# Lightning attention feeding a leaky-ReLU feed-forward block: the attention's small matmuls gathered into one TensorE visit per chunk, with the PSUM banks shared out anew

## The chip, the cores and the metric

One core of one Trainium2 chip runs the whole program. The metric is the device time of that core in microseconds (us): 662.45 us as the median of three runs of the kernel before (660.42 to 664.43). A separately profiled execution of it spans 662.8 us; all profile times below are counted from the start of that span.

## The reference

Two blocks follow each other. The attention works on blocks of 64 tokens with a decaying state; its output, 3072 tokens by 512 features, is the input of a feed-forward block with a leaky ReLU.

```
batch, heads, seq, head_dim = 4, 8, 768, 64          # block = 64 tokens
for each block b:
    intra = (q_b k_b^T * Dmask) v_b                   # within the block
    inter = (q_b * lam_pow) kv_state                  # from the blocks before
    out_b = intra + inter
    kv_state = lam**64 * kv_state + (k_b * rev_pow)^T v_b
x = out as (3072 tokens, 512)
h = x @ w_in            # 512 x 2048
g = max(0.01 h, h)
return g @ w_out        # 2048 x 512
```

The weights arrive as 64-bit floats and are converted on the chip.

## The kernel before

**Three products for one.** A 32-bit product is built from three products of TensorE's shorter 32-bit type (fp32r). An operand x is split into a high part xh and a rest xl, and a third operand xm is made of the two; the same for w. The first two products, h with h and l with l, are summed in one PSUM bank (`b1`), the third, m with m, goes to another (`b2`), and ScalarE and VectorE put the two sums together. For one half (`f`) of a pair of feature blocks `p` and one group `g` of 512 tokens this is 3 x 4 matmuls of 128x128 weights by 512 columns:

```python
def up(g, p):                                  # first layer, one of 48 steps
    ...
    for f in range(2):
        t, r = tt[jt], gs[jg][:, f, :]
        add("PE", 0.91, lambda f=f: product(b1, f, 0, True), keys("h"), ["b1"])     # 4 matmuls
        add("PE", 0.91, lambda f=f: product(b1, f, 1, False), keys("l"), ["b1"])    # 4 matmuls
        add("ACT", 0.6, lambda t=t: nc.scalar.activation(out=t, in_=b1, func=AF.Copy, ..., scale=1.0 + 1.0 / S), ["b1"], [f"t{jt}"])
        add("PE", 0.91, lambda f=f: product(b2, f, 2, True), keys("m"), ["b2"])     # 4 matmuls
        add("DVE", 0.69, lambda t=t, r=r: nc.vector.tensor_tensor(r, t, b2, op=ALU.add), [f"t{jt}", "b2"], [f"gs{jg}"])
    ...                                        # leaky ReLU on ScalarE, store to memory
```

**A planner in the kernel.** `add` only records an operation with its engine, a duration the author assumes, and the keys it reads and writes. At the end `plan.emit()` plays the list through, engine by engine, and emits the instructions in the order of that play. Each engine then runs its instructions in this fixed order; only semaphores hold it.

**Attention by chunks of 128 tokens** (24 chunks, two blocks each). A "quad" is a 64x64 by 64x64 matmul on a quarter of the array.

```python
pt = [ps([P, HP, C], f"pt{i}") for i in range(2)]      # two banks: transposes of k and q, later the state updates
psc = ps([P, 2, 2 * HP, C2], "psc")                    # two banks, scores in the lower half of each
po = ps([P, 2, 2 * HP, C2], "po")                      # two banks, outputs in the lower half of each
b1, b2 = ps([P, T], "b1"), ps([P, T], "b2")            # one bank each

def attention(c):
    ...                                                # loads of k, q, v (two buffers each)
    transposed(tk, 0, "k", kT)                         # PE: 4 transposes, ACT copies them out
    transposed(tq, 1, "q", qT)                         # PE: 4 transposes, ACT copies them out
    add("POOL", 1.15, ...)                             # k *= decay
    add(...)                                           # q * powers of lam
    add("PE", 0.56, scores, ...)                       # 16 quads into psc
    add("DVE", 0.69, ...)                              # sc = psc * mask
    add("PE", 0.56, kv, ...)                           # 16 quads: state updates, into pt[0], pt[1]
    add("PE", 0.56, own, ["sc", f"v{i}"], ["po"])      # 16 quads
    ...                                                # state = state + update (DVE), state * lam**64 (POOL)
    for n in range(2):
        add("PE", 0.3, lambda n=n: inter(n), ..., ["po"], rank=1.5 * n)      # 8 quads each
        if n == 0:
            add("DVE", 0.15, lambda: nc.vector.tensor_copy(seen_po, po[:, :, 0, 0]), ["po"], ["seen_po"])
    add("ACT", 0.6, ... scale=S)                       # xs = S * po
    add("ACT", 0.6, ... scale=NEAR)                    # xh = po rounded to fp32r
    add("DVE", 0.75, ...)                              # xl = xs - S * xh   (both from SBUF)
    add(("DVE", "POOL"), (0.75, 1.2), ... ALU.subtract)   # xm = xh - xl      (either engine)
```

Each of these PE entries is placed by itself, wherever the planner finds its inputs ready, between entries of `up`. The weights' parts `wl` may also be computed by either VectorE or GpSimd (`("DVE", "POOL"), (1.3, 2.3)`).

**Order of the whole.** Chunks 0 to 3 come first; then 48 steps `up(g, p)` with the other 20 chunks between them, in bursts of four as the two buffers of X come free; the eight w_in conversions lie ahead of the first steps, and the eight w_out conversions beside later ones; then the second layer (`down`), 1152 more matmuls of the same size.

Of the kernel before, what the change touches and what calls it, by code (L numbers as in the profile page):

```python
# [23 lines left out]

S = 4096.0
NEAR = 1.0 - 2.0 ** -13

# [6 lines left out]
class Plan:  # L34
# [6 lines left out]
    def __init__(self):  # L41
        self.ops, self.last, self.rank = [], {}, 0.0

    def add(self, eng, us, fn, reads=(), writes=(), rank=0.0):

        n, deps = len(self.ops), set()
        for k in reads:
            w, r = self.last.setdefault(k, [None, []])
            if w is not None:
                deps.add(w)  # L50
            r.append(n)
        for k in writes:
            w, r = self.last.setdefault(k, [None, []])
            if w is not None:
                deps.add(w)
            deps.update(r)
            self.last[k] = [n, []]
        deps.discard(n)
        ways = {eng: us} if isinstance(eng, str) else dict(zip(eng, us))
        self.ops.append((ways, fn, deps, (self.rank + rank, n)))  # L60

    def emit(self):
        n = len(self.ops)
        left = [len(o[2]) for o in self.ops]
# [20 lines left out]
        while len(done) < n:  # L85
            best = None
            for e in free:
                for i in able[e]:
                    t = max(free[e], since(i, e))
# [3 lines left out]
            ways, fn = self.ops[i][:2]  # L93
            for x in ways:
                able[x].discard(i)
# [15 lines left out]
def kernel(  # L111
# [39 lines left out]
    pt = [ps([P, HP, C], f"pt{i}") for i in range(2)]  # L151
    psc = ps([P, 2, 2 * HP, C2], "psc")
    po = ps([P, 2, 2 * HP, C2], "po")
    b1, b2 = ps([P, T], "b1"), ps([P, T], "b2")
# [3 lines left out]
    xs = [sb([P, KO, C], f"xs{i}") for i in range(2)]  # L158
# [35 lines left out]
    for _ in range(WARM):  # L194
        nc.tensor.transpose(out=b1[:, 0:P], in_=ident, identity=ident)
# [39 lines left out]
    def attention(c):  # L235
        b, s0, i = c // NCB, (c % NCB) * C, c % 2
        first, last = c % NCB == 0, c % NCB == NCB - 1
        tk, tq, tv = (x[i] for x in kqv)
        kT, qT, qsT = kTs[i], qTs[i], qsTs[i]

        pu = [(b1.rearrange("p (y t) -> p y t", y=HP), "b1"), (b2.rearrange("p (y t) -> p y t", y=HP), "b2")] if c < GC else [
            (pt[0], "pt0"), (pt[1], "pt1")]

        def load(src, dst, nm):
            y = src[b, :, s0:s0 + C, :]
            if nm == "v":
                add("DMA", 1.15, lambda: nc.sync.dma_start(out=dst, in_=y.rearrange("h p d -> p h d")), [], [f"v{i}"])
            else:
                def go():
                    for z in range(2):  # L250
                        nc.sync.dma_start(out=dst[:, z * HP:(z + 1) * HP, :], in_=y[z::2].rearrange("h p d -> p h d"))  # L251
                add("DMA", 1.15, go, [], [f"{nm}{i}"])

        for src, dst, nm in ((k, tk, "k"), (q, tq, "q"), (v, tv, "v")):
            load(src, dst, nm)

        def transposed(src, z, nm, into):
            def go():
                for y in range(HP):
                    nc.tensor.transpose(out=pt[z][:, y, :], in_=src[:, 2 * y:2 * y + 2, :].rearrange("p a d -> p (a d)"),  # L260
                                        identity=ident)
            add("PE", 0.45, go, [f"{nm}{i}"], [f"pt{z}"])
            add("ACT", 0.6, lambda: nc.scalar.copy(into, pt[z]), [f"pt{z}"], [f"{nm}T{i}"])

        transposed(tk, 0, "k", kT)
        transposed(tq, 1, "q", qT)
        kr = tk.rearrange("p (y x) d -> p y x d", x=2)
        nr = slice(0, C2 if last else P)
        add("POOL", 1.15, lambda: nc.gpsimd.tensor_tensor(kr[nr], kr[nr], _bc(pow_k, 3, D)[nr], op=ALU.mult),  # L269
            ["fk"], [f"k{i}"])  # L270

        m = slice(1 if first else 0, 2)
        o, x = (z.rearrange("p y (t i) -> p y t i", t=2)[:, :, m, :] for z in (qsT, pt[1] if c < GC else qT))
        eng, e, us, src = ("DVE", nc.vector, 0.7, "pt1") if c < GC else ("POOL", nc.gpsimd, 1.4, f"qT{i}")
        add(eng, us, lambda: e.tensor_tensor(o, x, _bc(pow_q, 2, 2)[:, :, m, :], op=ALU.mult), ["fq", src], [f"qsT{i}"])

        def scores():
# [4 lines left out]

        add("PE", 0.56, scores, [f"kT{i}", f"qT{i}"], ["psc"])
        add("DVE", 0.69, lambda: nc.vector.tensor_tensor(sc, psc[:, :, 0:HP, :], decay, op=ALU.mult), ["psc", "fk"], ["sc"])  # L284

        n_pu = 1 if last else 2

        def kv():
            for y in range(HP):
                for x in range(2):  # L290
                    for t in range(n_pu):
                        h = y // 2 + (2 * y + x) % HP * 2
                        quad(pu[t][0][:, y, 0:D], t, tk[:, 2 * y + x, :], tv[:, h, :], x, start=y == 0)

        add("PE", 0.56, kv, [f"k{i}", f"v{i}"], [pu[t][1] for t in range(n_pu)])
# [9 lines left out]
        def inter(n):  # L305
            for y in range(HP):
                t = y % 2 ^ n
                for hi in range(2):
                    if not first or t:
# [3 lines left out]
        add("PE", 0.56, own, ["sc", f"v{i}"], ["po"])  # L313
        for t in range(n_pu):
            j = 2 * c + t
            new = state[j % 4]
            if first and t == 0:
                add("DVE", 0.42, lambda new=new: nc.vector.tensor_copy(new, pu[0][0][:, :, 0:D]), [pu[0][1]], [f"st{j % 4}"])
            else:
                add("DVE", 0.42, lambda new=new, t=t: nc.vector.tensor_tensor(new, new, pu[t][0][:, :, 0:D], op=ALU.add),  # L320
                    [pu[t][1]], [f"st{j % 4}"])
            if not last:
                add("POOL", 0.7, lambda new=new, j=j: nc.gpsimd.tensor_tensor(state[(j + 1) % 4], new, _bc(lam_c, 2, D), op=ALU.mult),  # L323
                    [f"st{j % 4}", "fq"], [f"st{(j + 1) % 4}"])
            if t == 0:
                for n in range(2):
                    add("PE", 0.3, lambda n=n: inter(n), [f"qsT{i}", f"st{j % 4}"] + ([] if first else [f"st{(j - 1) % 4}"]), ["po"],
                        rank=1.5 * n)
                    if n == 0:

                        add("DVE", 0.15, lambda: nc.vector.tensor_copy(seen_po, po[:, :, 0, 0]), ["po"], ["seen_po"])
# [4 lines left out]
        y = po[:, :, 0:HP, :]  # L336
# [4 lines left out]
        def name(x):  # L341
            return f"x{x}{g % 2}"

        add("ACT", 0.6, lambda: nc.scalar.activation(out=tok(xs[i]), in_=y, func=AF.Copy, bias=0.0, scale=S), ["po"], [f"xs{i}"])
        add("ACT", 0.6, lambda: nc.scalar.activation(out=tok(xh), in_=y, func=AF.Copy, bias=0.0, scale=NEAR),  # L345
            ["po"], [name("h") + str(cc)])
        add("DVE", 0.75, lambda: nc.vector.scalar_tensor_tensor(xl, xh.bitcast(F32), -S, xs[i], op0=ALU.mult, op1=ALU.add),  # L347
            [name("h") + str(cc), f"xs{i}"], [name("l") + str(cc)])
# [226 lines left out]
```

## Time and profile before

| what | value |
|---|---|
| time, median of three | 662.45 us |
| TensorE busy (matmul) | 637.4 us, 96% |
| VectorE, ScalarE, GpSimd busy | 54%, 43%, 14% |
| first-layer matmuls (line 432) | 3 x 384, from 35.3 us on |
| second-layer matmuls (line 482) | 12 groups of 96 |
| transposes (line 260), quads (line 225) | 192 and 1472 + 768 + 576 + 128 records (two per quad) |
| mean granted TensorE clock | 0.983 of full; 0.86 in the first 50 us, 0.93 in the next 50, 1.00 after |

How to read it: matmuls overlap one another, and their ends are modelled, so the busy share of TensorE says little; the distance from one matmul's start to the next one's start says more. That distance is read from the timeline, whose lines give start, length, engine, source line, what is written from what, and how many instructions in a row were merged. An "idle before" in brackets names what ended a wait. "PEld" is the loading of weights into the array. A quad leaves two records, so x32 is 16 quads.

### The profile page before, as it was taken

How to read it: one execution, taken by the hardware profiler on the slowest of the kernel's cores; microseconds unless marked ns; L12 is line 12 of the kernel's file. 1: busy time of each engine (PE TensorE's matmuls, PEld its weight loads, DVE VectorE, ACT ScalarE, POOL GpSimd, SP SyncE). 2: the span in 40 equal slices, each digit the busy share in tenths (PEclk: the TensorE clock that was granted, in tenths of full speed). 3: DMA queues.
4: the chain of work that ended last, by engine and by line, in shares of the span. 5: the costliest groups of instructions: out<-in, count | busy, mean ns of one | idle time of the engine just before them, and what ended most of it. 6: DMA issues, size and time to landing. Idle time of an engine off the chain costs nothing.

```text
span 662.8 us, 13107 instructions
## 1 busy us (share of the span) xinstructions
PE 637.4 (96%) x5450; PEld 505.2 (76%) x5450; DVE 359.9 (54%) x481; ACT 285.8 (43%) x412; POOL 93.2 (14%) x96
## 2 busy tenths in 40 slices
PE   6688999999999999999999999999999999999997
PEld 5565767877677777777777778888888888888885
DVE  5777887555666234324326788363554544554631
ACT  5555778776776344453443353222231312222211
POOL 2542522311242124222200000000000000000000
PEclk8887999999999999999999999999999999999999
DMA  8855676877786435333243565252333332423201
GB/s 209 223 156 150 191 213 220 253 237 250 223 245 191 163 112 144 114 118 106 75 181 133 186 225 188 93 186 68 144 114 125 119 135 84 171 94 129 96 0 63
DMA packets 102090, 101.51 MB, mean 153 GB/s; under 512 B 78480, under 2 KB 78480, under 8 KB 102032
## 3 DMA queue, kind: packets, MB, share of 16 engines
q1 hardware_dynamic: 101888, 100.68, 48.5%
q8 instruction: 42, 0.69, 0.4%
q14 instruction: 16, 0.13, 0.1%
q10 hardware_dynamic: 144, 0.00, 0.0%
HBM read 65.02 MB, written 35.65 MB: 152 GB/s over the span
## 4 chain that ended last, share of the span: by engine, by line
PE 85%; DMA 4%; DVE 3%; ACT 3%; issue 2%; SPq 1%; POOL 0%; ACTq 0%; DVEq 0%; POOLq 0%
PE b L432 37%; PE po L482 10%; PE psc L482 10%; PE pt L482 10%; PE b L482 10%; PE po L225 3%; PE pt L260 2%; DMA raw<-in_moe_w_in_dram 2%; PE psc L225 2%; DMA wo<-w 1%; PE pt L225 1%; SPq L251 1%; DMA att<-in_v_dram 1%; DVE w L385 1%; DVE xm L349 1%
## 5 line engine op out<-in xcount | busy, mean ns | idle before, releaser
L446 DVE TENSOR_TENSOR gs<-t,b 128x512 f32<-128x512 f32 x96 | 65.8, 686 | 105.3 <-PE b L432 80.5
L432 PE MATMUL b<-xh,wh 128*128 128x512 f32 x384 | 114.4, 420 | 4.0 <-ACT xh L345 2.5
L467 ACT ACTIVATE xh<-att 128x1024 fp32r<-128x1024 f32 x48 | 50.8, 1061 | 144.1 <-PE po L482 141.0
L432 PE MATMUL b<-xm,wm 128*128 128x512 f32 x384 | 105.7, 398 | 4.7 <-DVE gs L446 3.1
L468 DVE SCALAR_TENSOR_TENSOR xl<-xh,att 128x1024 fp32r<-128x1024 f32 x48 | 58.6, 1221 | 93.7 <-ACT xh L467 93.7
L432 PE MATMUL b<-xl,wl 128*128 128x512 f32 x384 | 106.1, 398 | 0.9 <-DVE xl L347 0.9
L443 ACT ACTIVATE t<-b 128x512 f32<-128x512 f32 x96 | 57.2, 596 | 96.9 <-PE b L432 96.5
L432 PEld LDWEIGHTS b<-xm,wm 128*128 128x128 f32 x384 | 72.1, 190 | 21.2 <-DVE gs L446 3.5
L432 PEld LDWEIGHTS b<-xl,wl 128*128 128x128 f32 x384 | 71.6, 189 | 18.3 <-DVE xl L347 1.8
L432 PEld LDWEIGHTS b<-xh,wh 128*128 128x128 f32 x384 | 65.6, 190 | 23.7 <-ACT t L443 8.9
L448 ACT ACTIVATE gs<-gs 128x1024 f32<-128x1024 f32 x48 | 50.8, 1059 | 31.8 <-DVE gs L446 31.8
L470 DVE TENSOR_TENSOR xm<-xh,xl 128x1024 fp32r<-128x1024 f32 x48 | 58.8, 1225 | 4.8
L225 PEld LDWEIGHTS po<-att 64*64 64x64 f32 x1472 | 28.7, 140 | 24.2 <-issue 12.2
L225 PE MATMUL po<-att 64*64 64x64 f32 x1472 | 36.3, 231 | 6.2 <-DVE att L284 2.4
L269 POOL TENSOR_TENSOR att<-att 128x512 f32<-128x512 f32 (+1 forms) x24 | 27.9, 1161 | 100.0 <-PE pt L260 90.6
L323 POOL TENSOR_TENSOR att<-att 128x256 f32<-128x256 f32 x40 | 29.8, 746 | 73.0 <-DVE att L320 55.9
L482 PE MATMUL psc<-wm,xm 128*128 128x512 f32 x96 | 37.3, 389 | 0.0
L482 PE MATMUL po<-wh,xh 128*128 128x512 f32 x96 | 37.3, 389 | 0.0
L482 PE MATMUL pt<-wh,xh 128*128 128x512 f32 x96 | 37.3, 389 | 0.0
L482 PE MATMUL psc<-wl,xl 128*128 128x512 f32 x96 | 37.3, 389 | 0.0
L482 PE MATMUL b<-wl,xl 128*128 128x512 f32 x96 | 37.3, 389 | 0.0
L482 PE MATMUL b<-wm,xm 128*128 128x512 f32 x96 | 37.3, 389 | 0.0
(76 smaller groups left out, 935.0 us busy)
## 6 DMA issues: line engine op xcount, KB each, us to landing
g<-gs SPq DMA_DIRECT2D x48, 512.0 KB, 3.1
att<-g SPq DMA_DIRECT2D x48, 512.0 KB, 3.2
raw<-in_moe_w_in_dram SPq DMA_DIRECT2D x16, 512.0 KB, 4.5
raw<-in_moe_w_out_dram SPq DMA_DIRECT2D x16, 512.0 KB, 4.0
att<-in_k_dram SPq DMA_DIRECT2D x48, 128.0 KB, 3.3
att<-in_q_dram SPq DMA_DIRECT2D x48, 128.0 KB, 3.0
att<-in_v_dram SPq DMA_DIRECT2D x24, 256.0 KB, 3.7
out_dram<-gs SPq DMA_DIRECT2D x24, 256.0 KB, 2.2
```

What stands on the lines that cost most here:

```text
L225: nc.tensor.matmul(dst[HALF[cols]], lhsT=lhsT[HALF[rows]], rhs=rhs[HALF[rows]], start=start, stop=True, skip_group_check=True)
L260: nc.tensor.transpose(out=pt[z][:, y, :], in_=src[:, 2 * y:2 * y + 2, :].rearrange("p a d -> p (a d)"), identity=ident)
L269: add("POOL", 1.15, lambda: nc.gpsimd.tensor_tensor(kr[nr], kr[nr], _bc(pow_k, 3, D)[nr], op=ALU.mult), ["fk"], [f"k{i}"])
L323: add("POOL", 0.7, lambda new=new, j=j: nc.gpsimd.tensor_tensor(state[(j + 1) % 4], new, _bc(lam_c, 2, D), op=ALU.mult), [f"st{j % 4}", "f ...
L432: nc.tensor.matmul(dst, lhsT=w[z][:, kk * 2 * P + f * P:kk * 2 * P + (f + 1) * P], rhs=x[z][:, kk, :], start=start and kk == 0, stop=kk == ...
L443: add("ACT", 0.6, lambda t=t: nc.scalar.activation(out=t, in_=b1, func=AF.Copy, bias=0.0, scale=1.0 + 1.0 / S), ["b1"], [f"t{jt}"], rank=-1.5)
L446: add("DVE", 0.69, lambda t=t, r=r: nc.vector.tensor_tensor(r, t, b2, op=ALU.add), [f"t{jt}", "b2"], [f"gs{jg}"], rank=-1.5)
L448: add("ACT", 1.05, lambda: nc.scalar.activation(out=y, in_=y, func=AF.Prelu, bias=0.0, scale=S, alpha=0.01), [], [f"gs{jg}"], rank=-1.5)
L467: add("ACT", 1.05, lambda: nc.scalar.activation(out=h, in_=graw[j], func=AF.Copy, bias=0.0, scale=NEAR / S), reads, wr("h"))
L468: add("DVE", 1.3, lambda: nc.vector.scalar_tensor_tensor(l, h.bitcast(F32), -S, graw[j], op0=ALU.mult, op1=ALU.add), reads + [f"rh{j}"], w ...
L470: add(("DVE", "POOL"), (1.3, 2.3), lambda e: ENG[e].tensor_tensor(m, h.bitcast(F32), l.bitcast(F32), op=ALU.subtract), [f"rh{j}", f"rl{j}" ...
L482: nc.tensor.matmul(acc[tb][z // 2], lhsT=ring[j][z][:, f * T + tb * P:f * T + (tb + 1) * P], rhs=W[pp][z][:, f * d_model:(f + 1) * d_model ...
```

## The change

What it does, and what each part is for:

- **One visit per chunk.** The planner learns chains: PE entries between `begin` and `end` are emitted one after the other with no other PE work between them, once all that they need from outside is ready. `round_of(c)` makes such a chain: transposes of chunk c+2, `own` and the first half of `inter` of chunk c, scores and state updates of chunk c+1, the second half of `inter` of chunk c. The `seen_po` wait between the halves of `inter` has the 32 quads of the next chunk over it. Chunks 0 to 3 stay as they were (`alone`); `begun(4)` starts the pipeline.
- **Banks.** State updates move to the upper halves of `psc`, and the k transposes to the upper halves of `po`, so `pt` shrinks to one bank; the freed bank makes `b1` two banks, used in turn.
- **Scaled weights.** The weights carry a factor 2**16, `wh` one of 16; so xl is `po - xh` straight from PSUM, the copy `xs` on ScalarE goes, and the scale is taken out when the sums are put together. `xm`, `wl` and `wm` are computed by VectorE alone.

The core of the diff (cuts marked ...):

```diff
+U = 16.0
+WS = S * U
...
+        follows, heads = {}, {}
+        for c in self.chains.values():
+            m = [i for i in c if "PE" in self.ops[i][0]]
+            for i in c[1:]:
+                self.ops[m[0]][2].update(self.ops[i][2] - set(c))
...
+                    if e == "PE" and (i != locked[0] if locked else i in follows):
+                        continue
...
-    pt = [ps([P, HP, C], f"pt{i}") for i in range(2)]
+    pt = ps([P, HP, C], "pt")
-    b1, b2 = ps([P, T], "b1"), ps([P, T], "b2")
+    b1, b2 = [ps([P, T], f"b1{i}") for i in range(2)], ps([P, T], "b2")
-    xs = [sb([P, KO, C], f"xs{i}") for i in range(2)]
...
+        return [(psc[:, t, upper, :], "psc") for t in range(2)]
...
+            z, key = po[:, :, upper, :], "po"
...
+        add("PE", 0.61, own, ["sc", f"v{i}"], ["po"])
+        add("PE", 0.24, lambda: inter(0), needs, ["po"])
+        add(("DVE", "ACT"), (0.15, 0.25), lambda e: (nc.vector.tensor_copy if e == "DVE" else nc.scalar.copy)(seen_po, po[:, :, 0, 0]),
+            ["po"], ["seen_po"], rank=-3.0)
+        between()
+        add("PE", 0.46, lambda: inter(1), needs + ["seen_po"], ["po"])
...
-        add("ACT", 0.6, lambda: nc.scalar.activation(out=tok(xs[i]), in_=y, func=AF.Copy, bias=0.0, scale=S), ["po"], [f"xs{i}"])
-        add("DVE", 0.75, lambda: nc.vector.scalar_tensor_tensor(xl, xh.bitcast(F32), -S, xs[i], op0=ALU.mult, op1=ALU.add),
-        add(("DVE", "POOL"), (0.75, 1.2), lambda e: ENG[e].tensor_tensor(xm, xh.bitcast(F32), xl.bitcast(F32), op=ALU.subtract),
+            add("DVE", 0.7, lambda: nc.vector.tensor_tensor(tok(xl), y, tok(xh.bitcast(F32)), op=ALU.subtract),
+            add("DVE", 0.7, lambda: nc.vector.scalar_tensor_tensor(xm, xl.bitcast(F32), -S, xh.bitcast(F32), op0=ALU.mult, op1=ALU.add),
...
-        add(("DVE", "POOL"), (1.3, 2.3), lambda e: ENG[e].tensor_tensor(wl, src, wh.bitcast(F32), op=ALU.subtract),
+        add("DVE", 1.25, lambda: nc.vector.scalar_tensor_tensor(wl, wh.bitcast(F32), -S, src, op0=ALU.mult, op1=ALU.add),
...
-            add("PE", 0.91, lambda f=f: product(b1, f, 0, True), keys("h"), ["b1"])
+            t, r, b, kb = tt[jt], gs[jg][:, f, :], b1[jt], f"b1{jt}"
+            add("PE", 0.91, lambda f=f, b=b: product(b, f, 0, True), keys("h"), [kb])
...
+    def round_of(c):
+
+        after = []
+        if c + 2 < NCH:
+            load_kq(c + 2)
+        plan.begin(c)
+        if c + 2 < NCH:
+            after.append(transposes(c + 2))
+        after.insert(0, outputs(c, lambda: after.append(scores(c + 1)) if c + 1 < NCH else None))
+        plan.end()
+        for x in after:
+            x()
+        if c + 2 < NCH:
+            load_v(c + 2)
```

The work of the second layer and the number of matmuls, transposes and quads stay as they are.

## Prediction, made before the changed kernel was run

> **What bounds the kernel now.** I read the page first: TensorE is busy 96% of the span, no other engine over 54%, and the chain that ended last is 85% TensorE, 37% of the span on the first-layer line alone. So time must come out of TensorE's own sequence. But "busy" hides what lies between matmuls, so I went to TensorE's timeline in three places.
>
> Second layer, one line per matmul (start, length, what):
>
> ```profile
> 404.54 0.39 PE L482 MATMUL po<-wm,xm 128*128 128x512 f32 x1
> 404.76 0.39 PE L482 MATMUL po<-wh,xh 128*128 128x512 f32 x1
> 404.99 0.39 PE L482 MATMUL po<-wl,xl 128*128 128x512 f32 x1
> ```
>
> Starts lie 0.227 us apart; in the chain 12 such take 2.72 us. That is the floor. First layer, no attention near:
>
> ```profile
> 333.69 1.20 PE L432 MATMUL b<-xh,wh 128*128 128x512 f32 x4
> 334.73 1.08 PE L432 MATMUL b<-xl,wl 128*128 128x512 f32 x4
> 335.64 1.08 PE L432 MATMUL b<-xm,wm 128*128 128x512 f32 x4
> 336.56 1.19 PE L432 MATMUL b<-xh,wh 128*128 128x512 f32 x4
> ```
>
> The h group takes 1.04 us to the next start, l and m 0.91 and 0.92. So about 0.11 us is lost once per 12 matmuls, at the first h after an m: it writes `b1`, which ScalarE has only just emptied (the waits view has weight loads waiting on line 443 29 times, 8.9 us). First layer with attention between:
>
> ```profile
> 217.09 1.19 PE L432 MATMUL b<-xh,wh 128*128 128x512 f32 x4
> 218.12 1.08 PE L432 MATMUL b<-xl,wl 128*128 128x512 f32 x4
> 219.04 1.07 PE L432 MATMUL b<-xm,wm 128*128 128x512 f32 x4
> 220.04 0.69 PE L225 MATMUL pt<-att 64*64 64x64 f32 x32
> 220.66 1.19 PE L432 MATMUL b<-xh,wh 128*128 128x512 f32 x4
> ```
>
> From 217.09 to 220.04 is 2.95 us for 12 matmuls: 0.23 over the floor. The 16 quads (x32) take 0.62 us; elsewhere 32 quads in one visit take 1.09, so 16 cost 0.47 (29 ns each) and the visit 0.15. **A visit of quads costs about 0.37 us beyond its work.** A visit of transposes alone does not: 4 take 0.35, 8 take 0.79 us, so 4 cost 0.44 and the visit gives 0.09 back, about what is lost at re-entry.
>
> Counting changes of kind along the timeline from the first first-layer matmul at 35.3 us, I find 84 visits for 20 chunks: 67 begin with quads, 17 with transposes. With their 1,192 quads and 152 transposes (0.11 us each), the first-layer stretch of 361.9 us (to the last first-layer matmul, second-layer ones among them taken out) divides so:
>
> - 1152 matmuls x 0.2267: 261.1
> - the attention's work: 1192 x 0.0294 + 152 x 0.11 = 51.7
> - switching: 67 x 0.37 plus 17 x about 0.02 = 25.1
> - late h after m, 31 of them without a visit between, x 0.105: 2.6
> - the rest, 21.4: waits, the slow clock, about 3 of jitter
>
> Most of that rest lies before 100 us, where the granted clock is under 1. The worst case:
>
> ```profile
> 50.50 5.01 DVE L349 TENSOR_TENSOR xm<-xh,xl 128x512 fp32r<-128x512 f32 x1
> ...
> 56.16 1.80 PE L432 MATMUL b<-xm,wm 128*128 128x512 f32 x4 [3.12 <-DVE gs L446]
> ```
>
> VectorE's `xm` takes 5.01 us where the median is 0.69, while GpSimd runs three operations end to end (from 50.23: 1.15, 2.37, 1.27 us); TensorE waits 3.12 us behind it, and its next four matmuls take 1.80 instead of 1.07.
>
> **What the Trainium skill says.** (1) "TensorE: Matmul & The Clock Gate", section "Step-by-step: what each phase is for": weight loads are pulled ahead of running matmuls. The trace fits: loads of 188 ns vanish in the second layer's 227 ns, and the 0.11 us after a wait or a visit looks like a load that could not go early; nothing here proves that reading. (2) "SBUF — State Buffer", section "Who interferes with whom": a VectorE instruction with two SBUF inputs and a GpSimd one that reads SBUF exclude each other for the whole instruction. The 5.01 us agrees. After the change `xl` reads PSUM and one SBUF tile, so it is out of this; `xm` still has two SBUF inputs and is not. (3) "PSUM — Partial Sum Buffer", section "Summary: rules for kernel authors": guard PSUM by bank. That is why one `b1` makes h wait for ScalarE, and why chunks sharing `po` and `psc` must be emptied before the next visit.
>
> **The change, part by part** (us):
>
> 1. *One visit.* A visit is 8 transposes (0.79) and 64 quads (1.88), plus a change from one kind to the other inside (0.13, from the 8 visits that had one): about 2.8, less for first and last chunks of a sequence. It starts with transposes, before which nothing is lost, and loses 0.11 on the way back. Overhead per visit 0.13 - 0.09 + 0.11 = 0.15. For 20 rounds and three starting pieces (0.27 each): 3.8. Against 25.1: **-21.3**. All of it is on TensorE, which is the path.
> 2. *Second `b1`.* h writes the other bank, emptied long before; if the wait is the cause of the 0.105, all late h's go: **-2.6** (and there would now be some 70 of them, 7.4 us, if it is not).
> 3. *Scaled weights, no `xs`.* ScalarE loses 24 x 0.6 = 14 us at 43% load: off the path, except before group 0 and group 1 start, where ScalarE, VectorE and TensorE wait in turn. There it shortens the tail of a chunk by 0.5. **-1** for the start.
> 4. *No `wl`, `xm` on GpSimd; `xl` from PSUM.* Two `wl` (2.75 and 2.37) and three `xm` (1.29) leave GpSimd; stalls such as the 5.01 lose most of their cause. I take **-4** out of the 21.4.
> 5. *New waits in the visit.* `seen_po` must get from TensorE to VectorE or ScalarE and back within 32 quads, 0.94 us; it takes 0.15 to run, but may stand behind an operation of 0.69 or 1.22. Keys of k, q, v and the previous states all come due in one place, while loads take 3.0 to 3.7 us to land. I allow 0.15 per visit: **+3**.
> 6. *Weight conversion.* `wm` of the third and fourth pair came 5 to 7 us before their use (57.2 against 63.8; 71.6 against 76.7). TensorE gets there sooner by about that: **+2**.
> 7. *Second layer*: nothing changes (both of its scalings cost what they did, 1.22 each on VectorE): 0.
>
> Sum: -21.3 - 2.6 - 1 - 4 + 3 + 2 = -23.9, so 662.45 becomes about **638.5**; I say 638.
>
> **Rivals.** *A: the long visit starves the rest.* A chain is only let go when everything for it is ready, and five operations on each of ScalarE and VectorE then come due at once. For it: ScalarE would have about 6.3 us of work in the 8.3 us of a step and a chunk while w_out is converted (2 x 0.6 for t, 1.06, 3 x 0.6, 2.2). Against it: the rest of a step, 5.4 us of matmuls, lies between visits, and the 84 visits of before needed the same operations. If it held, waits of 0.5 to 0.8 us a visit would leave 648 to 655. *B: the weights bound the first 115 us.* The last `wm` of w_in ended at 116 us; if loading and conversion keep their pace, the early third of the gain is lost: about 645. Against it: the trace shows no TensorE wait on `wh`, `wl` or `wm`, and conversions stand in ScalarE's and VectorE's queues behind work that itself waits for TensorE, so they move up too. *C: switching costs are tied to the boundaries of quads, not of visits.* If transposes-to-quads, quads on `po` to quads on `psc` and back each cost 0.15, a visit has four of them, 20 x 0.6 = 12 back: 648. Against it: before, visits with psc and pt quads cost one 0.15 (1.09 for 32), and `own` with half of `inter` 0.86 for 24. *D: early waits go almost wholly*, another 6 us: 632.
>
> **Range and chances.** The switching term is counted, its unit read from dozens of equal cases; I trust it to 3 us. The waits are guesses of 5 to 8 us either way, D below and B or C above. So 627 to 650 eight times in ten. Faster by over 2% means under 649.2, which needs 13.3 of the 23.9 to come true: 0.88. Within 2%: 0.1. Slower by 2%: 0.02; two rivals would have to come together.
>
> **What the profile after would show.** If step 1 is right: about 20 long visits of near 2.8 us after 45 us, groups of 24 first-layer matmuls between them near 5.45 us, and quads at 29 ns. Step 2: no h group longer than l or m. Step 4: no `xl` over 0.7 us, few `xm` over 1. Step 5: in the waits, quads on `po` behind `seen_po` and quads on `psc` behind the v load; 3 us in all. Step 6: waits of first-layer matmuls on `wm`, 2 us. Step 7: the second layer at 0.227 a matmul and a tail of 4 us. The prediction is wrong if a visit takes over 3.3 us without a named wait, if the first first-layer matmul moves later than 36 us, or if TensorE waits over 10 us in the first 115.

## The result, and the profile after

The changed kernel takes **640.04 us** (median of four, 637.1 to 644.9), against 662.09 for the kernel before beside it: a ratio of 0.967 (95% interval 0.961 to 0.974). A second session gave 639.17 and 0.9635 (0.9606 to 0.9664). The prediction had 638.0 and a range of 627 to 650.

The profiled execution after spans 635.2 us. Where the prediction showed lines of the kernel before, these are the answers, all from the timeline (start, length, engine, line, what is written from what). Second layer:

```profile
404.34 0.39 PE L571 MATMUL b<-wh,xh 128*128 128x512 f32 x1
404.57 0.39 PE L571 MATMUL b<-wl,xl 128*128 128x512 f32 x1
```

Still 0.227 us from start to start, and 4.66 us from the last such start to the end, as before (4.65). First layer without attention near:

```profile
326.14 1.07 PE L519 MATMUL b<-xh,wh 128*128 128x512 f32 x4
327.05 1.07 PE L519 MATMUL b<-xl,wl 128*128 128x512 f32 x4
327.95 1.07 PE L519 MATMUL b<-xm,wm 128*128 128x512 f32 x4
328.86 1.07 PE L519 MATMUL b<-xh,wh 128*128 128x512 f32 x4
```

All four groups are alike now, 0.90 to 0.91 us to the next start; the h group had 1.04. And a whole visit of a chunk:

```profile
126.49 1.07 PE L519 MATMUL b<-xm,wm 128*128 128x512 f32 x4
127.40 0.60 PE L302 MATMUL po<-att 128*128 128x128 f32 x4
127.83 0.60 PE L302 MATMUL pt<-att 128*128 128x128 f32 x4
128.37 0.93 PE L253 MATMUL po<-att 64*64 64x64 f32 x48
129.11 1.11 PE L253 MATMUL psc<-att 64*64 64x64 f32 x64
130.05 0.41 PE L253 MATMUL po<-att 64*64 64x64 f32 x16
130.39 1.20 PE L519 MATMUL b<-xh,wh 128*128 128x512 f32 x4
131.42 1.07 PE L519 MATMUL b<-xl,wl 128*128 128x512 f32 x4
```

From 127.40 to 130.39 is 2.99 us. At 0.11 a transpose and 29.4 ns a quad the work is 8 x 0.11 + 64 x 0.0294 = 2.76, so 0.23 is lost inside; the h group after it takes 1.03 instead of 0.91, so 0.11 or 0.12 is lost on the way back. Nothing is lost on the way in (126.49 to 127.40 is 0.91).

**A ledger.** To compare kernels I divide the stretch from the first to the last first-layer matmul (second-layer ones among them taken out). The 1152 matmuls at 226.7 ns (261.1 us) and the attention's work (51.8 to 52.7) are the same everywhere. What is over divides by place. "Ends" is what the last matmul ahead of a visit and the first one after it lose, up to 0.15 each. "Inside" is a visit's time beyond its work. "Late h" is lost at an h after an m. "Between" is the rest, all the longer waits among it.

| kernel | time | ratio to before, 95% | visits (beginning with quads) | first matmul at | ends | inside | late h | between |
|---|---|---|---|---|---|---|---|---|
| before | 662.1 | 1 | 84 (67) | 35.3 | 15.5 | 20.1 | 2.6 | 10.8 |
| the change | 640.0 | 0.967 | 22 (2) | 33.2 | 3.4 | 11.8 | 0.1 | 7.3 |
| four_visits | 648.5 | 0.975 (0.971 to 0.979) | 86 (59) | 34.0 | 14.8 | 13.1 | 0.0 | 1.7 |
| two_visits | 637.2 | 0.961 (0.957 to 0.964) | 41 (21) | 34.3 | 7.2 | 11.5 | 0.1 | 3.6 |
| one_b1 | 650.5 | 0.980 (0.976 to 0.985) | 22 (2) | 33.2 | 3.2 | 13.1 | 7.3 | 9.4 |
| old_scaling | 636.3 | 0.959 (0.956 to 0.962) | 21 (2) | 36.0 | 3.4 | 9.3 | 0.1 | 4.9 |
| after_again | 639.2 | 0.964 (0.961 to 0.966) | 22 (2) | 33.5 | 3.3 | 11.9 | 0.1 | 8.3 |
| before_scaled | 657.6 | 0.991 (0.988 to 0.994) | 84 (66) | 36.5 | 15.2 | 13.6 | 2.8 | 8.6 |
| two_visits_old_scaling | 640.4 | 0.965 (0.963 to 0.968) | 41 (22) | 36.7 | 7.1 | 11.4 | 0.0 | 4.0 |
| planner_free | 634.3 | 0.956 (0.952 to 0.959) | 34 (13) | 35.2 | 5.3 | 10.3 | 0.0 | 3.1 |
| seen_po_dve | 633.9 | 0.955 (0.952 to 0.958) | 22 (2) | 32.9 | 3.6 | 10.3 | 0.0 | 6.8 |
| free_old_scaling | 640.8 | 0.968 (0.964 to 0.972) | 29 (7) | 36.4 | 4.0 | 13.1 | 0.2 | 4.4 |
| free_and_dve | 632.9 | 0.952 (0.949 to 0.955) | 32 (10) | 34.5 | 4.9 | 12.8 | 0.2 | 2.8 |

Times and ratios are of all executions of a kernel, the other columns of one profiled execution; kernels of one session ran on one chip, and the ratios are the safer thing to compare between sessions. The profiled executions of before and after lie 27.6 us apart in span, the medians 22.1: so the columns overstate this one difference by some 5 us (the profiled execution of before was a long one, 666.65 us against 660.4 to 664.4 for the others; that of the change was the shortest of its four). By the columns it came from the ends (12.1), the inside of visits (8.3), late h (2.5), between (3.5) and an earlier first matmul (2.1).

What went against the change is also in the timeline. Two visits of the same trace are much longer than 2.99 us. The first, TensorE and then ScalarE:

```profile
145.49 0.93 PE L253 MATMUL po<-att 64*64 64x64 f32 x48
146.24 1.11 PE L253 MATMUL psc<-att 64*64 64x64 f32 x64
148.80 0.46 PE L253 MATMUL po<-att 64*64 64x64 f32 x16 [1.45 <-ACT w L465]
```

```profile
145.70 0.69 ACT L465 ACTIVATE w<-raw 128x512 f32<-128x512 f32 x1 [1.28 <-DMA wo<-w]
146.29 1.04 ACT L536 ACTIVATE gs<-gs 128x1024 f32<-128x1024 f32 x1
147.24 0.13 ACT L385 COPY att<-po 128x2 f32<-128x2 f32 x1
147.28 0.57 ACT L312 COPY att<-pt 128x512 f32<-128x512 f32 x1
147.76 0.66 ACT L465 ACTIVATE w<-raw 128x512 f32<-128x512 f32 x1
```

The copy on line 385 is `seen_po`. Here the planner gave it to ScalarE, where it stands behind a weight conversion, which itself waited 1.28 us for a transfer, and behind a leaky ReLU of 1.04. I first read the 1.45 us as its doing. But it ended at 147.37, the last quad on psc had started at 147.13, and the last 16 records of quads start at 148.80: 1.4 us lie after `seen_po`, and the second conversion, which the profile names, is not what these quads need. The other long visit has the same gap in a plainer form:

```profile
184.06 0.41 PE L253 MATMUL po<-att 64*64 64x64 f32 x12
186.57 0.33 PE L253 MATMUL po<-att 64*64 64x64 f32 x4 [2.10 <-issue]
```

"issue" means that nothing in the profile released it. It falls in the middle of a planner entry, ahead of a quad that waits for no semaphore. What the two have in common is told in the last section; the experiments were made while I still held `seen_po` for the cause of the first.

### The profile page after: what moved, and what is told of

Same layout as the page of the kernel before. It is cut to its first block, busy times and chain, and to the rows that moved or that the text cites. A ratio compares the mean times of both kernels' runs of the same rounds, so it can differ in the third digit from the quotient of the medians.

```text
span 635.2 us, 13063 instructions
## 1 busy us (share of the span) xinstructions
PE 613.1 (97%) x5450; PEld 506.9 (80%) x5450; DVE 358.5 (56%) x475; ACT 274.9 (43%) x399; POOL 82.4 (13%) x91
## 4 chain that ended last, share of the span: by engine, by line
PE 88%; DVE 5%; DMA 3%; ACT 2%; issue 1%; SPq 0%; ACTq 0%; DVEq 0%
PE b L519 37%; PE b L571 17%; PE psc L571 10%; PE po L571 10%; PE pt L571 3%; PE po L253 3%; DMA att<-in_k_dram 3%; PE psc L253 2%; PE pt L302 2%; PE po L302 1%; DVE wl L483 1%; DVE w L472 1%; DVE xl L402 1%; DMA wo<-w 1%; DVE wh L480 0%
## 5 line engine op out<-in xcount | busy, mean ns | idle before, releaser
L533 DVE SCALAR_TENSOR_TENSOR gs<-b,t 128x512 f32<-128x512 f32 x96 | 66.2, 690 | 92.3 <-PE b L519 83.6
L556 DVE SCALAR_TENSOR_TENSOR xl<-att,xh 128x1024 fp32r<-128x1024 f32 x48 | 58.7, 1223 | 93.8 <-ACT xh L555 93.6
L519 PE MATMUL b<-xh,wh 128*128 128x512 f32 x384 | 105.0, 396 | 1.7 <-ACT xh L401 1.7
L519 PEld LDWEIGHTS b<-xh,wh 128*128 128x128 f32 x384 | 70.7, 188 | 17.4 <-ACT xh L401 2.2
L571 PE MATMUL b<-wh,xh 128*128 128x512 f32 x192 | 74.8, 389 | 0.0
L571 PE MATMUL b<-wl,xl 128*128 128x512 f32 x192 | 74.7, 389 | 0.0
L558 DVE SCALAR_TENSOR_TENSOR xm<-xl,xh 128x1024 fp32r<-128x1024 f32 x48 | 58.7, 1225 | 4.6
L253 PE MATMUL po<-att 64*64 64x64 f32 x1472 | 34.3, 227 | 9.7 <-DVE att L346 4.0
L571 PEld LDWEIGHTS b<-wh,xh 128*128 128x128 f32 x192 | 36.1, 188 | 7.6
L571 PEld LDWEIGHTS b<-wl,xl 128*128 128x128 f32 x192 | 36.0, 188 | 7.4
L253 PEld LDWEIGHTS po<-att 64*64 64x64 f32 x1472 | 28.2, 138 | 15.5 <-issue 6.1
L571 PE MATMUL psc<-wh,xh 128*128 128x512 f32 x96 | 37.4, 389 | 0.0
```

Of the source, the lines that this page charges most:

```text
L253: nc.tensor.matmul(dst[HALF[cols]], lhsT=lhsT[HALF[rows]], rhs=rhs[HALF[rows]], start=start, stop=True, skip_group_check=True)
L519: nc.tensor.matmul(dst, lhsT=w[z][:, kk * 2 * P + f * P:kk * 2 * P + (f + 1) * P], rhs=x[z][:, kk, :], start=start and kk == 0, stop=kk == ...
L533: add("DVE", 0.69, lambda t=t, r=r: nc.vector.scalar_tensor_tensor(r, b2, -1.0 / WS, t, op0=ALU.mult, op1=ALU.add), [f"t{jt}", "b2"], [f"g ...
L556: add("DVE", 1.25, lambda: nc.vector.scalar_tensor_tensor(l, graw[j], 1.0, h.bitcast(F32), op0=ALU.mult, op1=ALU.subtract), reads + [f"rh{ ...
L558: add("DVE", 1.25, lambda: nc.vector.scalar_tensor_tensor(m, l.bitcast(F32), -S, h.bitcast(F32), op0=ALU.mult, op1=ALU.add), [f"rh{j}", f" ...
L571: nc.tensor.matmul(acc[tb][z // 2], lhsT=ring[j][z][:, f * T + tb * P:f * T + (tb + 1) * P], rhs=W[pp][z][:, f * d_model:(f + 1) * d_model ...
```

## The experiments

**First: are visits what costs?** Two versions of the changed kernel with more visits. `two_visits` closes the chain between the halves of `inter`'s wait and opens another:

```diff
-        after.insert(0, outputs(c, lambda: after.append(scores(c + 1)) if c + 1 < NCH else None))
+        def between():
+            plan.end()
+            plan.begin((c, 1))
+            if c + 1 < NCH:
+                after.append(scores(c + 1))
+        after.insert(0, outputs(c, between))
```

`four_visits` drops the lock and names four pieces of a chunk (transposes; own and half of inter; scores and updates; the rest). Where first-layer work is ready, the planner may not let one piece follow another directly:

```diff
-                    if e == "PE" and (i != locked[0] if locked else i in follows):
+                    if e == "PE" and i in self.pieces and now not in (None, self.pieces[i]) and any(
+                            j not in self.pieces for j in able[e]):
                         continue
```

> The changed kernel with its chains dissolved: each round's TensorE work is cut in four pieces (transposes; own and half of inter; scores and state updates; the other half of inter) and the planner must put first-layer matmuls between two pieces. Banks and arithmetic stay as changed. 86 visits by the built order (59 begin with quads, 27 with transposes) in place of 22. Theory (each quad visit costs about 0.37 us beyond its work; in the changed kernel's profile a whole visit costs 0.23 inside and 0.11 after it): 59 x 0.37 + 27 x 0.02 - 22 x 0.34 = +15 us, so about 655 us. Rival 1 (the gain came from the second bank and from waits that went): under +5, 640 to 645. Rival 2 (spread pieces hide waits that the one visit has inside): +10 or less.

> The changed kernel with each round in two chains: transposes, own and the first half of inter; then scores, updates and the second half of inter, behind seen_po. 41 visits by the built order, 21 of them quads only. Theory (0.37 us a quad visit): 19 more visits, +7 us, about 647, less what the waits for seen_po inside the visit cost (2 us in the profile after), so +5 to +7. Rival (cost goes with the changes of kind inside the visit, not with visits): the same changes of kind happen in both, so within 2 us of the changed kernel, 640.

Measured: 648.46 and 637.24 us. More visits do cost more in the columns: 64 more than the change add 11.4 us at the ends in `four_visits`, 19 more add 3.8 in `two_visits`, 0.18 to 0.20 a visit both times. But "between" falls by 5.6 and 3.7. So the theory holds for the switching in kind and misses for both sums. `four_visits` is 5 to 8 us above the change by the ratios (8.4 by the medians) where 15 were expected; its second rival, that spread pieces hide waits, had it. `two_visits`, expected 5 to 7 us above, is at 0.961, not slower than the change. There the rival has the number nearly right, but not the reason: its visits did cost 3.8 us at the ends, and less waiting between visits made up for it. Which operations came sooner for it was not separated.

**Second: is it the one bank of sums?** `one_b1` is the changed kernel, writing one of its two banks only:

```diff
+    B1 = 0
-            t, r, b, kb = tt[jt], gs[jg][:, f, :], b1[jt], f"b1{jt}"
+            t, r, b, kb = tt[jt], gs[jg][:, f, :], b1[B1], f"b1{B1}"
```

> The changed kernel with first sums in one bank only (the second one stays unused in the first layer). Theory (each h group that follows an m group writes a bank that ScalarE has only just emptied and starts 0.105 us late): 76 such groups, +8 us, about 648; the timeline shows h groups of 1.04 us after m. Rival (the late start belongs to the change from m to h operands or banks): no change, 640, and then the changed kernel would not have lost its late h either. Rival 2 (with h, l, m of two halves no longer interleaved more waits follow): over +10.

Measured: 650.52 us, 9 to 11 more than the change, where 8 were expected. In its timeline the late h is back (1.03 or 1.04 us to the next start):

```profile
326.86 1.07 PE L520 MATMUL b<-xm,wm 128*128 128x512 f32 x4
327.77 1.20 PE L520 MATMUL b<-xh,wh 128*128 128x512 f32 x4
328.81 1.08 PE L520 MATMUL b<-xl,wl 128*128 128x512 f32 x4
```

and in its waits of weight loads (waited for: us in total, times, longest) there is a line that the change has not:

```profile
PEld b L520 <- ACT t L531: 22.3, 73, 1.3
```

76 late h's lose 7.25 us, 0.095 each. The wait of the h's weights for ScalarE's emptying of the same bank is the cause, and the second bank takes it away. The remaining 3 us lie inside visits and between (+1.3, +2.1).

**Third: what do the scaled weights bring?** `old_scaling` is the changed kernel with the arithmetic of before: `xs` on ScalarE, xl from SBUF, `wl` and `xm` on either engine:

```diff
+            add("ACT", 0.6, lambda: nc.scalar.activation(out=tok(xs[i]), in_=y, func=AF.Copy, bias=0.0, scale=S), ["po"], [f"xs{i}"])
-            add("DVE", 0.7, lambda: nc.vector.tensor_tensor(tok(xl), y, tok(xh.bitcast(F32)), op=ALU.subtract),
+            add("DVE", 0.75, lambda: nc.vector.scalar_tensor_tensor(xl, xh.bitcast(F32), -S, xs[i], op0=ALU.mult, op1=ALU.add),
...
-        add("DVE", 1.25, lambda: nc.vector.scalar_tensor_tensor(wl, wh.bitcast(F32), -S, src, op0=ALU.mult, op1=ALU.add),
+        add(("DVE", "POOL"), (1.3, 2.3), lambda e: ENG[e].tensor_tensor(wl, src, wh.bitcast(F32), op=ALU.subtract),
```

> The changed kernel with the arithmetic of before: weights unscaled, the scaled copy xs on ScalarE, xl from two SBUF tiles, xm and wl on VectorE or GpSimd as the planner likes. Visits and banks as changed. Theory (scaled weights were worth 1 at the start and 4 in stalls between VectorE and GpSimd): +5 us, 645, with xm or wl operations of 2 us and more in the profile before 100 us. Rival (those stalls move elsewhere, since two-input VectorE operations and GpSimd still meet in the changed kernel: wm 2.21, wl 1.96 us there): within 2 us, 640.

Measured: 636.31 us, less than the change, where the theory wanted 5 more and the rival no difference of over 2. Taken alone that says the scaling is worth nothing. So the next session ran the change once more, both departures together, and the converse edit: the kernel before with the scaled weights and nothing else (`before_scaled`, the same lines the other way round, 84 visits).

> The changed kernel once more, beside the next three kernels on one chip. Its time should be 0.967 of the kernel before, within 0.007. If it comes out at 0.959 to 0.962, where the version with the old scaling and the version with two visits stood, those two were no better than the change; if it stays at 0.967 or above, each of them saves 3 to 5 us.

> Both in one kernel: chunks in two visits, and the old scaling with GpSimd's share of the subtractions. Theory (each is better than the change by itself, for different reasons: work between the halves covers the waits inside a visit; GpSimd takes load off VectorE): 633 to 635 us, 3 to 5 below the better of the two. Rival (the differences were scatter between chips): within 2 us of the changed kernel beside it.

> The kernel before with the scaled weights alone: no xs, xl from PSUM, wl, xm and wm on VectorE alone; 84 visits, one b1 and all banks as before. The prediction's steps 3 and 4 (no copy on ScalarE, no stall of VectorE beside GpSimd): 5 us less than before, ratio 0.9925, and no xm of 5 us. Rival (what GpSimd no longer does, VectorE does, and the waits only move): within 2 us of before, ratio 0.997 to 1.003, as the old scaling in the changed kernel already hinted.

Measured: 639.17, 640.37 and 657.59 us. The change comes out at 0.9635, between the two outcomes named beforehand. So `old_scaling` is likely the faster of the two, by some 3 us, but the intervals touch (0.956 to 0.962 and 0.961 to 0.966). With two visits the old scaling costs about 3 us (0.961 to 0.965, and again the intervals touch); its rival, within 2 us of the change, was right. In the kernel before, the new scaling saves 5.9 (ratio 0.991, 0.988 to 0.994), as the prediction's steps 3 and 4 had it. The instructions of xm on VectorE in `before_scaled` (count, shortest/median/longest in ns):

```profile
L349 DVE SCALAR_TENSOR_TENSOR xm<-xl,xh x24: 681/692/1429, 14.8 to 321.6; 128x512 fp32r<-128x512 f32 x24
```

The longest is 1.43 us where before had 5.01. If the sign turns at all, it turns only in the locked version, so something else about that version had to be in the way.

**Fourth: is it the lock?** `planner_free` is the changed kernel with banks, scaling and order as they are and its chains left open:

```diff
-        self.chain = name
-        self.chains[name] = []
+        self.chain = None
```

> The changed kernel with its chains left open, so that the planner places every TensorE entry by itself: 34 visits in place of 22, 13 of them beginning with quads in place of 2. By the switching cost of about 0.2 us for a visit's two ends, and another 0.1 where it begins with quads: 12 x 0.2 + 11 x 0.1 = 3.5 us more than the changed kernel, less 1 to 2 us of waits inside visits: 642 us where that has 640. Rival (waits inside visits weigh as much as visits): no difference of over 1 us.

Measured: 634.30 us, 0.9555 against 0.9635 for the change on the same chip. The expectation had the wrong sign. Twelve more visits do cost 2.0 us at the ends, but inside and between fall by 1.6 and 5.2. The longest waits of TensorE with the lock (after_again) and without (planner_free), from the waits (columns as above), some of the start left out:

```profile
PE po L253 <- issue: 2.9, 1, 2.9
PE b L519 <- ACT xh L401: 1.7, 2, 1.0
...
PE b L519 <- DVE gs L533: 1.6, 1, 1.6
...
PE po L253 <- ACT w L465: 1.2, 1, 1.2
PE b L519 <- DVE xl L402: 1.1, 1, 1.1
```

```profile
PE b L518 <- ACT xh L400: 1.3, 2, 0.7
PE po L301 <- DMA att<-in_k_dram: 1.0, 1, 1.0
PE po L252 <- issue: 1.0, 1, 1.0
...
PE b L518 <- DVE gs L532: 0.5, 2, 0.3
```

The rank of the operations gathers most of a chunk by itself: 34 visits, not 84. The lock, which adds the last 12, costs more than it saves. In these two traces the difference lies in two places: the gaps in the middle of a visit (1.4 and 3.1 us in after_again; the longest here is 1.3, behind a load of k) and the waits of first-layer matmuls at 66 to 78 us (1.6, 1.0 and 1.1 in after_again against 0.2 and 0.6). Part of a round in planner_free, at the place of the longer gap:

```profile
183.47 0.93 PE L252 MATMUL po<-att 64*64 64x64 f32 x48
184.22 0.65 PE L252 MATMUL psc<-att 64*64 64x64 f32 x32
184.79 1.19 PE L518 MATMUL b<-xh,wh 128*128 128x512 f32 x4
185.92 0.46 PE L252 MATMUL po<-att 64*64 64x64 f32 x16
```

Four first-layer matmuls stand where the locked visit had its gap (the "issue" line of planner_free belongs to 15 us, ahead of the first layer).

**Fifth: which part of the lock?** Three versions. `last_half_free` ends the chain ahead of the second half of inter (`plan.end()` in the place of `between`, after the scores). `seen_po_dve` keeps the whole lock and takes from the planner only the choice of ScalarE:

```diff
-        add(("DVE", "ACT"), (0.15, 0.25), lambda e: (nc.vector.tensor_copy if e == "DVE" else nc.scalar.copy)(seen_po, po[:, :, 0, 0]),
+        add("DVE", 0.15, lambda: nc.vector.tensor_copy(seen_po, po[:, :, 0, 0]),
```

`free_old_scaling` has open chains and the old scaling.

> The changed kernel, with the chain ending ahead of the second half of inter: those 16 quads may go in wherever the planner finds them ready, after first-layer matmuls if need be. 32 visits in place of 22, 12 beginning with quads, 10 of them of 4 or 8 quads alone. Theory (the lock costs by the waits in the middle of a visit, 1.65 + 2.31 + 0.48 us in the changed kernel's trace, all of them ahead of these quads): they go, 10 more visits cost 10 x 0.25 = 2.5, so 1.5 to 2.5 us less than the changed kernel, ratio about 0.961. Rival (the lock costs by holding back the whole chain until the last of its inputs is there): no gain, 1 to 3 us slower than the changed kernel, ratio 0.965 to 0.968.

> The changed kernel with seen_po on VectorE only, as it was before the change; same 22 visits. Theory (in-visit waits come of seen_po standing behind ScalarE's weight conversion): the 1.4 to 1.65 us wait at 147 us goes, the one of 2.3 to 3.1 at 184 us, whose seen_po already ran on VectorE, stays: 1.5 us less, ratio 0.961. Rival (VectorE's queue is no shorter): within 1 us of the changed kernel, 0.9635.

> The old scaling in the kernel with open chains: 29 visits, 7 beginning with quads. Theory (the scaled weights save what they saved alone in the kernel before, 5.8 us, and did nothing in the locked version only because the lock's waits hid it): 638 to 640 us, ratio 0.962 to 0.964 against 0.9555 with the new scaling. Rival (with the visits gathered, the stalls that the scaling removes no longer lie on the path): 633 to 635, ratio 0.954 to 0.957.

Measured: 0.960 (0.9575 to 0.9626), 633.87 us (0.9549) and 640.75 us (0.968). The profiled execution of `last_half_free` was disturbed (a granted clock of 0.56), so only its other times count; they fit its theory, although the interval leaves the size of the gain open.

`seen_po_dve` saves 5.3 us by the medians where 1.5 was expected. The gap at 147 us is gone from its trace and the one of 184 us stays (1.6 us), just as the theory had it; but the theory can't be right, for `seen_po` was done 1.4 us before that gap ended. What differs at that place is that the visit waited 1.5 us for its k before it began. The spans of the profiled executions differ by 2.3 to 3.5 us, 1.5 of it inside visits. So the gain is measured, and its cause is not shown: with the choice taken away, the planner orders ScalarE and VectorE otherwise from there on.

`free_old_scaling` settles the scaling for open chains: there the scaled weights save 6.5 us by the medians and 8 by the ratios (0.956 against 0.968, intervals well apart), at least as much as in the kernel before.

Last, both edits together (`free_and_dve`), the candidate for the best:

> Open chains and seen_po on VectorE only, together: 32 visits, 10 beginning with quads. Theory (the two cure the same wait: with open chains nothing waited for seen_po, though ScalarE did 8 of 24): they do not add up, 633 to 635 us, ratio 0.954 to 0.957. Rival (open chains save by not holding back the start of a chain, VectorE's seen_po by shortening the visit, so that both count): 629 to 631, ratio about 0.949.

Measured: 632.92 us, 0.952 (0.949 to 0.955). That lies between the theory (0.954 to 0.957) and the rival (0.949), and the interval overlaps that of either edit alone. Had both gains added up in full, the ratio would be about 0.947, just outside the interval; whether they add up in part (1 to 1.5 us by the medians) stays open. By its median this is the fastest of the thirteen kernels, some 7 us below the change, and it is the changed kernel with two edits: no lock, and `seen_po` on VectorE. Its profiled execution, the slowest of its six (635.9 against 630.2 to 634.2), has a gap of 3.2 us at 186 us: those gaps do not belong to the lock alone.

## Why the prediction was right, and where it was not

The sum was right to 2 us, with several errors in it that cancel; that it came so near is in part luck.

- **Step 1, one visit (-21.3): right in kind, too large, its terms mis-sized.** (a) "A visit of quads costs about 0.37 us beyond its work": by `four_visits` against `planner_free`, which differ by the rule on pieces alone, 46 more visits that begin with quads (52 more visits in all) cost 9.5 us at the ends and 2.8 inside, 0.27 each, and 13 by the ratios, 0.29 each. (b) "Overhead per visit 0.13 - 0.09 + 0.11 = 0.15": measured 0.23 + 0.11 = 0.34, 3.8 us more over 20 visits. The -0.09 was the wrong term. It was the end of a visit of transposes alone, taken for its beginning; a visit that ends with quads does not get it back, and loses 0.13 at its last quad, which the sum left out (in the visit shown the last record of a quad takes 0.148 us to the next start where the others take 0.015 on average). The change from transposes to quads took 0.09 where 0.13 was counted. (c) Fewer visits alone bring far less than 21.3. `before_scaled` and `four_visits` have the same scaling and nearly the same number of visits (84 and 86), and yet lie some 10 us apart by the ratios (0.991 and 0.975): by the columns 6.9 between visits, 2.8 at late h's and 2.5 at the start. So that much comes from the rest of the change (the second bank, the attention's other banks, the order of a round), of which only the second bank was tried alone. From the 86 visits to the 22 of the change the ratios give 5 to 8 us more, to the 34 of planner_free some 13. All that together, from `before_scaled` to planner_free, is 23.3 us by the medians, near the 23.9 of steps 1 and 2; but by the columns only 13.2 of it lie at the ends and inside visits, where step 1 had 21.3.
- **Step 2, second b1 (-2.6, or +7.4 if the wait were not the cause): right.** The 31 late h's lost 2.64, now 0.1; `one_b1` puts 76 back for 7.25.
- **Steps 3 and 4, scaling and GpSimd (-5 together): right in the sum, and hidden in the changed kernel.** 5.9 alone on the kernel before, 6 to 8 with open chains. The 1 us at the start was not seen on its own: in `before_scaled` the first first-layer matmul came later (36.5 us against 35.3). In the change itself no xl lasted over 0.694 us and no xm over 0.703. The Trainium skill's "SBUF — State Buffer", section "Who interferes with whom", has VectorE and GpSimd exclude each other where VectorE reads two operands from SBUF; the xl with one operand in PSUM agrees. xm was said to stay exposed, and was not hit here; `wm` was, though GpSimd does nothing for the weights any more (VectorE and TensorE, timeline of the change):

```profile
62.91 2.21 DVE L485 SCALAR_TENSOR_TENSOR wm<-wl,wh 128x1024 fp32r<-128x1024 f32 x1
65.04 0.68 DVE L533 SCALAR_TENSOR_TENSOR gs<-b,t 128x512 f32<-128x512 f32 x1
65.78 0.96 PE L519 MATMUL b<-xm,wm 128*128 128x512 f32 x3 [1.65 <-DVE gs L533]
```

  GpSimd runs from 60.29 and from 62.15 (1.50 and 1.89 us), `wm` takes 2.21 instead of its median 1.22, and the sum `gs` behind it frees `b2` late.
- **Step 5, waits in the visit (+3): too small, and mostly not the waits it named.** In the quads of the change after 35 us the trace has 0.5 us at 298.42, behind `seen_po` in the last chunk, which has no other quads over it, and 1.65 and 2.3 us in gaps that no step had. `seen_po` did stand behind two operations, as feared, and ended some 0.2 us after the start of the last quad that covers it; its own cost is of that size. The wait for the v load did not come; those for k loads did, 0.5 us in all. What the lock costs as a whole, 4.9 us by `planner_free`, is more than the 3.
- **Step 6, weight conversion (+2): a wait of about that size, by another way.** No first-layer matmul waited for `wm`. What came was the 1.65 above, through VectorE's queue and `b2`.
- **Step 7, second layer: right**, 0.227 a matmul.
- **The rivals.** A (the long visit starves the rest) has something of the truth that its numbers missed: the lock loses 5 us, not 10 to 17. C (each change of kind costs) put 0.6 on a visit, the prediction 0.15; 0.34 is about halfway. D (early waits go almost wholly): TensorE's waits between 33 and 115 us, added up from the waits view, fell from 9.1 us to 4.3 in the change (5.5 in its second trace) and to 2.1 with open chains. Step 4 had already counted 4 of these, so D's further 6 did not come. B did not come.
- **The signs of being wrong.** Two of the three came up to the letter, though the number was right. A visit took over 3.3 us without a named wait: the one from 181.10 took 5.73, with the 2.10 shown above. TensorE waited over 10 us in the first 115: 13.3, of which 9.0 lie ahead of the first layer; this sign was badly set, since the kernel before has 17.9 there. The third, a first first-layer matmul later than 36 us, did not come (33.2).

Still open: why `old_scaling` seems to beat the change by 3 us while the old scaling costs 3 to 8 in three other structures. It loses 2.5 us less inside visits and has neither of the two gaps, so its order missed them; whether by rule or by luck no run tells. And why `seen_po` on VectorE is worth 5.3. And what part of the 10 us that came without fewer visits belongs to the attention's banks, and what part to the order of a round.

## What to carry to other kernels

Gathering small matmuls between large ones pays 0.2 us for the two ends of each visit saved, and some more inside; ordering by rank alone took 84 visits to 34 here, and a lock that forces the last 12 together lost more in waits than it saved. A change of several parts needs a run that undoes the part in its name and nothing else: with the visits put back (`four_visits`), more than half of the gain stayed. Where a large matmul follows a wait for its bank, a second bank is worth about 0.1 us each time. An edit judged inside one version can come out with the wrong sign (the scaling: -6, -6 to -8, about -3 and about +3 us in four structures, the last two with intervals that touch): try it in the kernel before as well, and do not build a theory on differences of 3 us between two orders of one planner.

## What the runs showed of the hardware that I had not expected

**TensorE seems to wait for its own instructions.** The 2.10 us at 186.57 has no releaser. The profile's table of DMA queues has this line for the change:

```profile
q8 instruction: 43, 0.70, 0.4%
```

43 packets of 16,384 bytes. The Trainium skill's "TensorE: Matmul & The Clock Gate", section "Step-by-step: what each phase is for", gives a matmul instruction 64 bytes; so a packet holds 256, and 43 hold 11,008, against 10,900 matmuls and weight loads in the trace. That fits TensorE's own stream, fetched while it runs. The gap at 186.57 ended 1.5 us after such a packet had landed (184.17 + 0.93 = 185.10, by the trace's DMA records). In the first 400 us of thirteen traces there are 15 places where one quad follows another over 0.35 us later without a semaphore to wait for. They are 0.5 to 3.4 us long, and **all 15 ended 1.32 to 1.60 us after the landing of a packet of this queue**, which come 8 to 11 us apart at the median. The gap at 148.80 ended 1.44 after one, 1.46 in the second trace of the change. Twelve of the 15 lie at three places of the sequence, in nine traces of changed kernels: at matmul record 221 or 222, 2000 to 2004, or 2635 to 2638, counted from 0. A packet holds 128 records with their weight loads, and the places agree with that as well: divided by 128, the record numbers of all 15, those of the kernel before and of `one_b1` among them, leave 75 to 94 (94 for 222, 90 for 602, 85 for 1365, 78 for 2638), falling slowly along the program. The gap at 148.80, record 2002, leaves 82.

A visit uses 2 x (128 + 8) = 272 instructions in 3 us, more than a packet, where 24 first-layer matmuls use 48 in 5.6 us. So gathering quads also gathers the demand for instructions, and the first-layer matmuls between quads in planner_free, at 184.79 above, leave time for a fetch (there a packet landed at 184.32, 1.6 us ahead of the quads at 185.92). The transfers were dense besides. For the 6 us around the gap of the change the same table reads:

```profile
q1 hardware_dynamic: 1877, 2.00, 102.7%
q8 instruction: 1, 0.02, 1.0%
```

Data transfers filled all sixteen engines, and one instruction packet went among them. That these gaps are late fetches is a reading: 15 coincidences in time and place support it, and no run moved the packets to prove it. If it holds, and with the gap at 148.80 and its like counted in, they cost 4.0 and 4.4 us ahead of the second layer in the two traces of the change.

**The cost of an end.** A 128x512 matmul ahead of a quad lost 0.09 to 0.10 us (6.4 us for 67 of them in before, 1.24 for 13 in planner_free), one ahead of a transpose 0.01 at the median; the first one after any visit lost 0.11 (2.4 us for the 22 of the change).
